# Where the row maximum of the attention scores is kept: an SBUF tile of its own, or a spare column of the scores' PSUM tile

## The chip, the cores and the metric

The kernel runs on 1 core of one Trainium2 chip. The metric is the device time of one execution in microseconds (us); several runs are taken and their median is compared. All times below come from those runs or from one profiled execution of the kernel.

## What is computed

Three layers follow each other over 4 batches of 576 tokens with 512 features. The first is attention with 8 heads of 64 features and a threshold: only scores within tau of the maximum of their row count.

```python
scores = scale * np.matmul(q, k.transpose(0, 1, 3, 2))
thresh = np.max(scores, axis=-1, keepdims=True) - tau
scores = np.where(scores >= thresh, scores, -1000000000.0)
attn = softmax(scores); x = np.matmul(attn, v)
```

Then each token goes through one of 8 experts (a gate picks one, or keeps the previous token's; two matrix products with a relu between, scaled by the expert's probability), and last through a normalised feed-forward layer with a residual. The change is in the attention alone.

## The kernel before, in words

Products are made on TensorE (PE) from float16 pairs (a high and a low part of each number). Attention goes pair of heads by pair of heads: 16 pairs (4 batches, 4 pairs each), nine *items* in each, 144 items in all. An item is 128 rows of queries against the 576 keys of their batch. Its scores are one PSUM tile `t` of the pool `ps_s`, 128 partitions by 2 by 512 float32 numbers. That is two banks, of which columns 0 to 287 are used in each. The pool has three such tiles.

The steps of an item, with their engine and the line of the code:

- `s_mm` (L342, L350, PE): the scores, four matmuls of 288 columns or twelve smaller ones.
- `mx` (L353 to L356, VectorE, DVE): the row maximum `m` of the 2 by 288 scores, by one reduction (L355).
- `bias` (L361, ScalarE, ACT): a copy of `m`, scaled, into column 0 of the small SBUF tile `bt`.
- `ex` (L367, ACT): the exponential `e` of the scores `t`, with `bt[:,0:1]` as bias.
- `thr` (L372, DVE): `bt[:,1:2] = m + ntau`, one number per partition; `ntau` is a constant in SBUF.
- `mask` (L382, for the odd item also L384, DVE): `em = (t >= threshold) * e`.
- `hilo` (L389 on ACT, L390 on GpSimd, POOL): `em` in two float16 parts `hl`.
- `tr` (L396): `hl` transposed by a DMA to `ht`, issued by SP; `pv` (L414 to L416, PE): times v; `norm` (L424, L428, L434, DVE): divided by the sum.

The order in which each engine gets its instructions is written out by hand in the loop that ends the kernel's attention part (L1038 to L1100). In step `it` of that loop `mx`, `bias` and `ex` belong to item `it`, then come `mask` of item `it - 1`, `thr` of item `it`, `hilo` of `it - 1` and `s_mm` of `it + 1`:

```python
if live: mx(*items[it])
...
    bias(*items[it])
...
    ex(*items[it])
if 0 < it <= NI:
    mask(*items[it - 1])
    if live: thr(*items[it])
```

So DVE's queue reads mx(it), mask(it-1), thr(it), other work, mx(it+1). ACT's reads bias(it), ex(it), hilo(it-1), other work, bias(it+1). Each engine takes its own queue strictly in order; between engines, semaphores hold an instruction until what it needs is there. The other work is dealt out by item number: scaling and splitting q, k and v of coming pairs (L295 to L329: ACT and POOL), narrowing of the feed-forward weights from 64-bit words (L154, L156, L158 on DVE, L169 and L176 on ACT, L170 on POOL), `norm`, the gate of a finished pair (L453 to L479) and, once a batch, the routing (L484 to L581, many small DVE operations). After the attention the experts and the feed-forward layer follow (L1103 to L1181), in which the change touches nothing.

Of the kernel before, what the change touches and what calls it, by code (L numbers as in the profile page):

```python
# [19 lines left out]
def kernel(  # L20
# [36 lines left out]
    x_d = dram.tile([NT, DM], F32, name="x_d")  # L57
    ys_d = dram.tile([NT, DM + 1], F32, name="ys_d")

# [1 line left out]
    ident = const.tile([128, 128], F32, name="ident")  # L61
    make_identity(nc, ident)
    ident16 = const.tile([128, 128], F16, name="ident16")
# [64 lines left out]
    nc.vector.tensor_tensor(out=taus, in0=t0, in1=ge, op=ALU.add)  # L128
    nc.vector.memset(c16, 16.0)

# [1 line left out]
    fw1 = fw_p.tile([128, 2, DM // 128, FF], F16, name="fw1")  # L132
    fw2 = fw_p.tile([128, 2, FF // 128, DM], F16, name="fw2")

# [4 lines left out]
    FA = 11  # L139

    def ffn_views(j):
        """1024 columns of float64 weights, as pairs of int32 words: source, place and scale."""
        if j < 8:
            c, o = j // 2, 1024 * (j % 2)
            src = w_ch1[128 * c:128 * c + 128, o:o + 1024].rearrange("p (a b) -> p a b", a=2)
            return src, fw1[:, :, c, o:o + 1024].rearrange("p t (a b) -> p t a b", a=2), g32[:, c:c + 1]
        j -= 8
        src = w_ch2[256 * j:256 * j + 256, :].rearrange("(c p) f -> p c f", p=128)
        return src, fw2[:, :, 2 * j:2 * j + 2, :], 64.0

    def narrow(t, r):
        """float64 words t to float32 r, in steps."""
        lo, hi = t[..., 0], t[..., 1]
        nc.vector.tensor_scalar(out=r, in0=hi, scalar1=3, scalar2=0x3FFFFFF8, op0=ALU.logical_shift_left, op1=ALU.bitwise_and)  # L154
        yield
        nc.vector.scalar_tensor_tensor(out=r, in0=hi, scalar=-(1 << 30), in1=r, op0=ALU.bitwise_and, op1=ALU.bitwise_or)  # L156
        yield
        nc.vector.scalar_tensor_tensor(out=r, in0=lo, scalar=29, in1=r, op0=ALU.logical_shift_right, op1=ALU.bitwise_or)  # L158
        yield

    def ffn_steps(j, a, cv_p):
        """the steps that load and split half of a part."""
        src, dst, scale = ffn_views(j)
        t = cv_p.tile([128, 512, 2], I32, name="stg")
        r = cv_p.tile([128, 512], I32, name="cv")
        rf = r.bitcast(F32)

        def low():
            nc.scalar.activation(out=dst[:, 0, a], in_=rf, func=AF.Copy)  # L169
            nc.gpsimd.tensor_tensor(out=dst[:, 1, a], in0=rf, in1=dst[:, 0, a], op=ALU.subtract)  # L170

        n = narrow(t, r)
        yield nc.sync.dma_start(out=t.rearrange("p b w -> p (b w)"), in_=src[:, a].bitcast(I32))
        for _ in range(3):
            yield next(n)
        yield nc.scalar.activation(out=rf, in_=rf, func=AF.Copy, scale=scale)  # L176
        yield low()

    def ffn_half(j, a):
        """the same for half of the columns; returns the step that follows the load."""  # L180
        src, dst, scale = ffn_views(j)
        t = P["sm2_p"].tile([128, 512, 2], I32, name="stg", tag="stg")
        nc.sync.dma_start(out=t.rearrange("p b w -> p (b w)"), in_=src[:, a].bitcast(I32))

        def run():
            r = P["n_p"].tile([128, 512], I32, name="xn", tag="xn")
            for _ in narrow(t, r):
                pass
            yield
            r = r.bitcast(F32)  # L190
            nc.scalar.activation(out=r, in_=r, func=AF.Copy, scale=scale)
            nc.scalar.activation(out=dst[:, 0, a], in_=r, func=AF.Copy)
            nc.gpsimd.tensor_tensor(out=dst[:, 1, a], in0=r, in1=dst[:, 0, a], op=ALU.subtract)

        return run()
# [1 line left out]
    P, wt = {}, {}  # L197

    def weights(u, n):
        """the tile of a unit's first (0) or second (1) weights."""  # L200
        if (u, n) not in wt:
            sh = [128, 2, DM // 128, F] if n == 0 else [128, 2, F // 128, DM]
            nm = f"w{n}{u % 2}"
            wt[u, n] = P["wb_p" if u % 2 else "wa_p"][n].tile(sh, F16, name=nm, tag=nm)
        return wt[u, n]

    def unit_part(u, j, p, ev):
        """loads the j-th eighth of a unit's weights; returns the step that splits it."""
        one = bass.ds(ev, 1) if not isinstance(ev, int) else slice(ev, ev + 1)
        t = p.tile([128, F], F32, name="stg", tag="stg")  # L210
        if j < 4:
            nc.sync.dma_start(out=t, in_=w1[one, 128 * j:128 * j + 128].rearrange("o p f -> p (o f)"))
            return lambda: split(weights(u, 0), t, j, 64.0)
        j -= 4
        t = t.rearrange("p (b f) -> p b f", f=DM)
        nc.sync.dma_start(out=t, in_=w2[one, 256 * j:256 * j + 256].rearrange("o (c p) f -> p (o c) f", p=128))
        return lambda: split(weights(u, 1), t, slice(2 * j, 2 * j + 2), 64.0)

    # ================= attention and routing =================
    R = dict(side="right")  # L220
    c_raw, c_tab, c_unit, c_tail, c_cv, c_pv, c_main = (ExitStack() for _ in range(7))
    tm = pool(c_tab, "tm", 1, **R)
# [19 lines left out]
    if True:  # L242
# [30 lines left out]
        pending, ops = {}, {}  # L273

        def load(b, nm, part):
            """one of four transfers of a batch's q, k or v."""
            src = {"q": q, "k": k, "v": v}[nm][b]
            o, m = (6, 1) if nm == "v" else (5, 0)
            t = raws[nm]
            if part < 2:  # L280
                n = NP // 2
                (nc.scalar if b else nc.sync).dma_start(
                    out=t[:, n * part:n * part + n].rearrange("p n (h r) d -> p (n h) (r d)", h=2)[:, :, 0:4 * D],
                    in_=src[2 * n * part:2 * n * part + 2 * n, 0:512].rearrange("h (p r) d -> p h (r d)", r=4))
            else:
                ab = part - 2
                (nc.scalar if b else nc.sync).dma_start(
                    out=t[64 * ab:64 * ab + 64, :, 4 + ab * m, :],
                    in_=src.rearrange("(n a) s d -> a s n d", a=2)[ab, 512:S])
# [61 lines left out]
            mst[s, ab] = t  # L351

        def mx(s, ab):  # L353
            m = sm_p.tile([128, 1], F32, name="m")
            nc.vector.tensor_reduce(out=m, in_=mst[s, ab][:, :, 0:288], op=ALU.max, axis=AX.XY)  # L355
            mst[s, ab] = (mst[s, ab], m)  # L356

        def bias(s, ab):
            t, m = mst[s, ab]
# [85 lines left out]
            nc.scalar.dma_start(out=x_d[b * S + 512:b * S + S, cols], in_=xc[0:64, 4, :])  # L445

        def bank(b):
            """a bank for small products; at the end, when there are more, one of those."""
            if b == B - 1 and "pa" in P:
                return P["pa"].tile([128, 4, 128], F32, name="a")  # L450
            return ps_t.tile([128, 4, 128], F32, name="t")

        def gate(p):  # L453
            """x of a head pair, transposed, for the logits."""
            b, hp = divmod(p, NP)
            xc = xcs[p]
            xt = xts[p % 2]
# [24 lines left out]
                yield from route(b)  # L482

        def route(b):  # L484
            """experts, their probabilities and places of a batch's tokens."""
            lg, e1 = lgs[b % 2], e1s[b % 2]
            T = lambda nm, sh, dt=F32: rt_p.tile(sh, dt, name=nm)
            V = nc.vector
# [92 lines left out]
                early_tables()  # L581

        def early_tables():
            """tables of the first tiles of two experts, without the last batch."""
            V = nc.vector
            V.tensor_scalar(out=etb, in0=acc[:, 0, 0:2], scalar1=OFF + NT / 2, scalar2=None, op0=ALU.add)
            V.tensor_scalar(out=etp, in0=acc[:, 1, 0:2], scalar1=2.0 ** -33, scalar2=None, op0=ALU.mult)
# [39 lines left out]
        for b in range(1, B):  # L627
            for o, a in zip(LO, (("q", 0), ("k", 0), ("v", 0), ("q", 2), ("q", 3), ("k", 2), ("k", 3), ("v", 2), ("v", 3), ("q", 1), ("k", 1), ("v", 1))):
                at(36 * (b - 1) + o, load, b, *a)
    # ================= tables of the units =================  # L630
    V = nc.vector

    def static_tables():
# [86 lines left out]
        V.tensor_scalar(out=P["tb"][:, 2 * E:NC], in0=A[:, 0:NDYN], scalar1=OFF + NT / 2, scalar2=None, op0=ALU.add)  # L720
        V.tensor_scalar(out=P["tp"][:, 2 * E:NC], in0=A[:, NDYN:2 * NDYN], scalar1=2.0 ** -33, scalar2=None, op0=ALU.mult)

    # ================= experts and feed-forward =================
    parts, wsel, us = {}, {}, {}

    PAIRS = {"a": (0, 1), "b": (2, 3)}

    def tiles(u):
        """table columns of a unit: two tiles of an expert's first rows, or one tile."""
        if u in PAIRS:  # L730
            return PAIRS[u]
        return (2 * u, 2 * u + 1) if u < E else (E + u,)
# [12 lines left out]
            us[u, "g"].append(xg)  # L745

    def fetch(u, j):
        """the j-th eighth of a unit's weights."""
        if u not in wsel:
            if u < E:  # L750
                wsel[u] = u
# [23 lines left out]
    late = []  # L775

    def drip(n=1):
        """splits the next parts of the weights, and loads ahead."""
        if late:
            next(late.pop(), None)  # L780
        for _ in range(n):
# [15 lines left out]
            more()  # L797

    def pace(u, share):
        """a share of the steps up to the end of a unit's part of the queue."""  # L800
        n = 0
        for k in pq:
            if k[0] != "f" and (k[0] - u) * 8 + k[1] > (7 if u < 6 else 11):
# [12 lines left out]
        us[u, "x"] = P["u_p"].tile([128, 2, 2, 4, 128], F16, name="xT")  # L816

    def t_unit(u):
        """x of a unit's tokens, transposed on the tensor engine."""
        new_x(u)  # L820
        x = us[u, "x"]
        for n, xg in enumerate(us.pop((u, "g"))):
# [4 lines left out]
            V.scalar_tensor_tensor(out=x[:, 1, n], in0=t, scalar=64.0, in1=x[:, 0, n], op0=ALU.mult, op1=ALU.subtract)  # L827

    def n_unit(u):
        """x of a unit's tokens in two float16 parts."""  # L830
        xs = us.pop((u, "g"))
        xn = P["n_p"].tile([128, 2, 2, DM], F16, name="n16")
        for n, xg in enumerate(xs):
# [2 lines left out]
        us[u, "n"] = xn  # L836

    def x_unit(u):
        """and transposed by the DMA engines."""
        new_x(u)  # L840
        x, xn = us[u, "x"], us.pop((u, "n"))
        if not single(u):
# [3 lines left out]
                nc.sync.dma_start_transpose(out=x[:, a, 0], in_=xn[:, a, 0])  # L846

    def s1_steps(u, k):
        """a part of the first product: as many columns as a bank holds."""
        x = us[u, "x"]  # L850
        two = u in PAIRS
        i, k = divmod(k, 2) if two else (0, k)
# [55 lines left out]
            pass  # L908

    def early_work():  # L910
        """the first tiles of two experts, in steps."""
        t_unit("a")
        yield
        for _ in range(4):
# [85 lines left out]
    NG = NT // 256  # L1000

    def halve(h):
        """half of the work of two sorted tiles."""
        g, b = divmod(h, 2)
        if b == 0:
            for fb in range(8):
# [204 lines left out]
```

## Time and profile before

| | us |
|---|---|
| median of 3 runs | 1118.63 |
| fastest and slowest run | 1113.96, 1120.94 |
| span of the profiled execution, first to last instruction | 1116.4 |
| attention: first and last row maximum start | 18.9, 421.5 |

For the profiled execution only its span is given, not a time of its own. The median of the runs is 2.2 us above the span; the span plus that is taken as the time of the profiled execution.

In the rows below, a group of instructions is one line: line of the code, engine, operation, names of what it writes and reads, shapes, count, busy time in us, mean duration of one in ns, and the idle time of the engine just before them with what ended it. Rows of the timeline begin with start and duration in us; an idle time before the instruction and what ended it stand in square brackets. A successor can start some hundredths before the predecessor's end, since engines overlap them.

### The profile page before, as it was taken

Reading aid. Unit: us, or ns where it says so; the run is one execution under the profiler, and the core shown is the slowest. Engines: PE = TensorE matmul, PEld = TensorE weight load, DVE = VectorE, ACT = ScalarE, POOL = GpSimd, SP = SyncE. Lnnn points to the kernel's source line nnn. Section 1 sums busy time; section 2 is a strip of 40 time slices with the busy share of each in tenths; the row PEclk is TensorE's granted clock in tenths of the full one; section 3 lists DMA queues with packets and bytes.
Section 4 is the critical chain, followed back from the end, with each engine's and each line's share of the span. In section 5 each row is a group of like instructions: output and inputs, shape, how many; then the busy total and the mean of one; then the engine's idle time right before and its main releaser. Section 6 shows DMA issues by size and latency. Waiting matters only on the chain. (4 is left out here: it accounts for less than half of the span.)

```text
span 1116.4 us, 20698 instructions
## 1 busy us (share of the span) xinstructions
PE 908.6 (81%) x8136; PEld 645.9 (58%) x8136; DVE 690.3 (62%) x1321; ACT 536.7 (48%) x930; POOL 382.7 (34%) x329
## 2 busy tenths in 40 slices
PE   1667575766577677878998879999989999999997
PEld 0446453645456566555666548667575675675673
DVE  4989789999998985876557665647230321321320
ACT  4868676877588764544557554435120111110110
POOL 3768675777577661132223221110100000000000
PEclk9767775887588877998999998999999999999999
DMA  7999999999999989648879887646111102101100
GB/s 201 203 217 226 213 220 211 202 233 222 197 192 209 189 174 266 228 121 268 291 231 307 251 233 234 177 134 195 64 43 43 29 29 57 29 29 58 29 11 19
DMA packets 314075, 181.02 MB, mean 162 GB/s; under 512 B 259179, under 2 KB 280683, under 8 KB 313969
## 3 DMA queue, kind: packets, MB, share of 16 engines
q1 hardware_dynamic: 283296, 150.08, 58.3%
q10 hardware_dynamic: 25712, 15.36, 5.4%
q0 software_dynamic: 4960, 14.17, 3.7%
q8 instruction: 65, 1.06, 0.4%
q14 instruction: 42, 0.34, 0.1%
HBM read 100.17 MB, written 15.22 MB: 103 GB/s over the span
## 5 line engine op out<-in xcount | busy, mean ns | idle before, releaser
L390 POOL TENSOR_TENSOR hl<-em,hl 128x576 f16<-128x576 f32 x144 | 193.5, 1346 | 114.6 <-ACT hl L389 103.9
L991 PE MATMUL y<-fw,hid 128*128 128x512 f16 x864 | 190.8, 383 | 3.5 <-ACTq L1163 3.5
L978 PE MATMUL a<-nT,fw 128*128 128x256 f16 x1728 | 190.1, 273 | 0.0
L978 PEld LDWEIGHTS <-fw 128*128 128x128 f16 x1728 | 169.1, 98 | 21.5
L869 PE MATMUL a<-xT,w 128*128 128x128 f16 (+1 forms) x1536 | 131.4, 250 | 34.9 <-DMA xT<-n 30.6
L137 DVE SCALAR_TENSOR_TENSOR w<-stg,w 128x1024 f16<-128x1024 f32 x112 | 136.3, 1238 | 32.8 <-ACT w L136 31.9
L414 PE MATMUL o<-vh,ht 128*128 128x65 f16 (+1 forms) x790 | 106.4, 218 | 57.3 <-DMA ht<-hl 32.6
L981 ACT ACTIVATE hid<-a 128x512 f16<-128x512 f32 x72 | 42.7, 593 | 219.2 <-PE a L978 219.2
L869 PEld LDWEIGHTS <-w 128*128 128x128 f16 x1536 | 118.5, 103 | 49.7 <-DMA xT<-n 34.0
L991 PEld LDWEIGHTS <-hid 128*128 128x128 f16 x864 | 85.3, 99 | 106.2 <-issue 7.5
L342 PE MATMUL s<-qkt 128*128 128x288 f16 x256 | 90.1, 362 | 57.1 <-DVE em L382 25.7
L414 PEld LDWEIGHTS <-ht 128*128 128x128 f16 (+1 forms) x800 | 89.8, 116 | 71.8 <-DMA ht<-hl 41.6
L382 DVE SCALAR_TENSOR_TENSOR em<-s,bt,e 128x576 f32<-128x576 f32 x144 | 115.6, 803 | 20.4 <-POOL hl L390 12.2
L996 POOL DMA_INDIRECT out_dram<-xf x18 | 18.9, 1049 | 317.1 <-DVE xf L995 317.1
L136 ACT ACTIVATE w<-stg 128x1024 f16<-128x1024 f32 x112 | 113.8, 1047 | 16.6 <-DMA stg<-in_moe_w_dram 12.6
L890 PE MATMUL y<-w,hid 128*128 128x512 f16 x528 | 118.8, 383 | 0.3 <-DVE w L137 0.3
L355 DVE TENSOR_REDUCE m<-s 128x1 f32<-128x576 f32 x144 | 107.3, 745 | 6.3 <-PE s L342 6.0
L982 DVE SCALAR_TENSOR_TENSOR hid<-a,hid 128x512 f16<-128x512 f32 x72 | 49.5, 688 | 99.3 <-ACT hid L981 97.8
L389 ACT ACTIVATE hl<-em 128x576 f16<-128x576 f32 x144 | 98.1, 681 | 23.3 <-DMA ht<-hl 16.4
L367 ACT ACTIVATE e<-s,bt 128x576 f32<-128x576 f32 x144 | 106.6, 740 | 4.7
L342 PEld LDWEIGHTS <-qkt 128*128 128x128 f16 x512 | 53.6, 121 | 94.6 <-DVE em L382 42.9
L995 DVE SCALAR_TENSOR_TENSOR xf<-y,xf 128x512 f32<-128x512 f32 x18 | 12.5, 692 | 153.1 <-PE y L991 153.1
(253 smaller groups left out, 1440.4 us busy)
## 6 DMA issues: line engine op xcount, KB each, us to landing
stg<-in_moe_w_dram SPq DMA_DIRECT2D x112, 512.0 KB
stg<-in_moe_w_ch_dram SPq DMA_DIRECT2D x32, 512.0 KB
xf<-ys_d SPq DMA_DIRECT2D x9, 513.0 KB
ku<-qkt SPq DMA_DIRECT2D x30, 144.0 KB
x_d<-xc ACTq DMA_DIRECT2D x16, 256.0 KB
rawq<-in_q_dram ACTq DMA_DIRECT2D x6, 512.0 KB
rawk<-in_k_dram ACTq DMA_DIRECT2D x6, 512.0 KB
vraw<-in_v_dram ACTq DMA_DIRECT2D x6, 512.0 KB
```

Source lines behind the costliest of these rows:

```text
L136: nc.scalar.activation(out=dst[:, 0, n], in_=t, func=AF.Copy, scale=scale)
L137: nc.vector.scalar_tensor_tensor(out=dst[:, 1, n], in0=t, scalar=scale, in1=dst[:, 0, n], op0=ALU.mult, op1=ALU.subtract)
L342: nc.tensor.matmul(t[:, c, 0:288], w, kk[:, 576 * ab + 288 * c:576 * ab + 288 * c + 288], start=(n == 0), stop=(n == 1))
L355: nc.vector.tensor_reduce(out=m, in_=mst[s, ab][:, :, 0:288], op=ALU.max, axis=AX.XY)
L367: nc.scalar.activation(out=e, in_=t[:, :, 0:288], func=AF.Exp, bias=bt[:, 0:1], scale=SC)
L382: nc.vector.scalar_tensor_tensor(out=o, in0=t[:, :, 0:288], scalar=th, in1=e, op0=ALU.is_ge, op1=ALU.mult)
L390: nc.gpsimd.tensor_tensor(out=hl[:, 1, c], in0=em[:, c], in1=hl[:, 0, c], op=ALU.subtract)
L414: mm(o[:, 0:65], ht[:, 0, j, sl], vh[:, jv, 0:65], start=(c == 0), stop=False)
L869: nc.tensor.matmul(ps[:, f, :], t1[:, a, c, fc], x[:, h, i:i + N // 128, c, :], start=(n == 0), stop=(n == 11))
L890: nc.tensor.matmul(ps, hid[:, x, f, 128 * i:128 * i + 128], t2[:, a, f, :], start=(n == 0), stop=(n == 23))
L978: nc.tensor.matmul(ps[:, f, :], fw1[:, a, c, fc], x[:, h, :, c, :], start=(n == 0), stop=(n == 11))
L991: nc.tensor.matmul(ps, hid[:, x, f, ts_], fw2[:, a, f, :], start=(n == 0), stop=(n == 47))
```

## The change

The maximum `m` is no longer a tile of the SBUF pool `sm_p`; it is the last column, 511, of the second bank of the item's own scores tile, which no matmul writes and no other step reads. The reduction writes there; `bias` (ACT) and `thr` (DVE) read it there. `sm_p` has one kind of tile less; nothing else is moved.

```diff
         def mx(s, ab):
-            m = sm_p.tile([128, 1], F32, name="m")
-            nc.vector.tensor_reduce(out=m, in_=mst[s, ab][:, :, 0:288], op=ALU.max, axis=AX.XY)
-            mst[s, ab] = (mst[s, ab], m)
+            t = mst[s, ab]
+            m = t[:, 1, 511:512]
+            nc.vector.tensor_reduce(out=m, in_=t[:, :, 0:288], op=ALU.max, axis=AX.XY)
+            mst[s, ab] = (t, m)
```

The rest of the diff takes out comments and docstrings.

## Rows read from the trace of the kernel before

**Rows 1.** The page of the profile: its first line
```profile
span 1116.4 us, 20698 instructions
```

**Rows 2.** Busy time by stretch, the attention: stretch, length, PE, PEld, DVE, ACT, POOL, clock, DMA share, GB/s
```profile
18.00:425.00 407.00, 269.49 (x3286) 209.49 (x3286) 370.98 (x774) 302.96 (x597) 279.05 (x214) 0.74 1.07 209
```

**Rows 3.** Groups of instructions of the whole span, by line
```profile
L355 DVE TENSOR_REDUCE m<-s 128x1 f32<-128x576 f32 x144 | 107.3, 745 | 6.3 <-PE s L342 6.0
L367 ACT ACTIVATE e<-s,bt 128x576 f32<-128x576 f32 x144 | 106.6, 740 | 4.7
...
L372 DVE TENSOR_TENSOR bt<-m,ntau 128x1 f32<-128x1 f32 x144 | 75.6, 525 | 0.0
...
L361 ACT ACTIVATE bt<-m 128x1 f32<-128x1 f32 x144 | 28.5, 198 | 63.1 <-DVE m L355 62.5
```

**Rows 4.** One line's instructions, L372: shortest, median, longest in ns, first and last start
```profile
L372 DVE TENSOR_TENSOR bt<-m,ntau x144: 138/476/1264, 19.7 to 422.9; 128x1 f32<-128x1 f32 x144
```

**Rows 5.** Timeline of DVE, ends of the nine items from 240.07, one whole
```profile
240.07 0.74 DVE L355 TENSOR_REDUCE m<-s 128x1 f32<-128x576 f32 x1
...
248.26 0.74 DVE L355 TENSOR_REDUCE m<-s 128x1 f32<-128x576 f32 x1
248.93 0.80 DVE L382 SCALAR_TENSOR_TENSOR em<-s,bt,e 128x576 f32<-128x576 f32 x1
249.66 1.15 DVE L372 TENSOR_TENSOR bt<-m,ntau 128x1 f32<-128x1 f32 x1
250.73 0.19 DVE L479 TENSOR_TENSOR lg<-t,lg 128x45 f32<-128x45 f32 x1
250.84 0.74 DVE L355 TENSOR_REDUCE m<-s 128x1 f32<-128x576 f32 x1
...
262.45 0.74 DVE L355 TENSOR_REDUCE m<-s 128x1 f32<-128x576 f32 x1
```

**Rows 6.** Timeline of POOL beside the whole item of rows 5
```profile
249.43 1.35 POOL L329 TENSOR_TENSOR vl<-vraw,vh 128x640 f16<-128x640 f32 x1
250.74 1.27 POOL L390 TENSOR_TENSOR hl<-em,hl 128x576 f16<-128x576 f32 x1
```

**Rows 7.** Timeline of ACT beside the whole item of rows 5
```profile
249.04 0.20 ACT L361 ACTIVATE bt<-m 128x1 f32<-128x1 f32 x1 [0.65 <-DVE m L355]
249.27 0.74 ACT L367 ACTIVATE e<-s,bt 128x576 f32<-128x576 f32 x1
249.91 0.67 ACT L389 ACTIVATE hl<-em 128x576 f16<-128x576 f32 x1
251.62 0.20 ACT L361 ACTIVATE bt<-m 128x1 f32<-128x1 f32 x1 [1.03 <-DVE m L355]
```

**Rows 8.** Single lines of DVE: shortest, median, longest in ns, first and last start
```profile
L434 DVE TENSOR_TENSOR xc<-o,rd x47: 273/410/425, 45.7 to 434.3; 128x256 f32<-128x256 f32 x32, 64x128 f32<-64x128 f32 x15
...
L479 DVE TENSOR_TENSOR lg<-t,lg x10: 192/193/195, 114.3 to 424.4; 128x45 f32<-128x45 f32 x10
...
L424 DVE TENSOR_SCALAR rd<-o x47: 138/145/163, 44.1 to 433.9; 128x4 f32<-128x4 f32 x32, 64x2 f32<-64x2 f32 x15
...
L158 DVE SCALAR_TENSOR_TENSOR cv<-stg,cv x22: 676/1386/1651, 32.1 to 310.7; 128x512 int32<-128x512 int32 x22
```

**Rows 9.** Two lines of ACT, from PSUM and from SBUF: ns, first and last start
```profile
L462 ACT ACTIVATE xt<-t x15: 576/585/597, 74.6 to 425.4; 128x512 f32<-128x512 f32 x15
...
L176 ACT ACTIVATE cv<-cv x6: 612/612/619, 245.5 to 314.4; 128x512 f32<-128x512 f32 x6
```

**Rows 10.** Who waited for whom, 60 to 420 us: us in total, times, longest
```profile
ACT bt L361 <- DVE m L355: 50.9, 56, 2.5
...
ACT hl L389 <- DMA ht<-hl: 16.4, 5, 6.4
...
ACT nat L301 <- DMA qkt<-nat: 8.3, 2, 4.5
```

## The prediction, made before the changed kernel was run

> **What bounds the kernel now.** I read the page first, then busy time by stretch, then the groups of instructions, then single lines and the timelines of DVE, ACT and POOL for one pair of heads, and last the waits. The span is 1116.4 us [rows 1], and the part that the change touches is the attention, 18 to 425 us. There DVE is busy 371.0 of 407 us (91%), ACT 303.0 (74%), POOL 279.1 (69%), PE 269.5; the DMA engines show a share of 1.07, so their queues are hardly ever empty [rows 2]. DVE sets the pace: in the nine items from 240.07 its rows follow each other without a gap (the whole item shown in [rows 5] is an example), while ACT stands idle before L361 until DVE's maximum is there, 50.9 us in 56 waits [rows 10]. The expert stage behind starts when the attention is done, so what the attention gains or loses moves the end one for one.
>
> Within DVE one row is odd. L372, an addition of one number per partition, takes 138 ns at best, 476 at the median and 1264 at worst [rows 4]; its 144 instructions add up to 75.6 us [rows 3]. In the item shown it starts at 249.66, takes 1.15 and ends at 250.81; POOL's operation beside it ends at 249.43 + 1.35 = 250.78 [rows 5, 6]. I laid all 144 against POOL's timeline: 87 last 0.2 us or more, and 83 of these end within 0.06 us of the end of a POOL operation. So an L372 that meets a running POOL operation waits for its end, inside its own duration. Both its inputs, m and ntau, lie in SBUF. L479 and L434 are additions and products of the same kind with one input in PSUM and one in SBUF: 192 to 195 ns, and 410 at the median with 425 at most [rows 8], never stretched, although the L479 shown starts at 250.73 just as POOL's next operation does [rows 5, 6].
>
> **The change part by part.**
>
> *The stretched additions go.* With m in PSUM L372 is like L479. 144 x 0.138 = 19.9 us stay of 75.6; -55.7 us on DVE's queue.
>
> *Their reading from PSUM.* L424 reads PSUM, 4 elements, in 145 ns at the median [rows 8] against 138: +7 ns, 144 times, +1 us. The bounds are -1 and, by its longest 163 ns, +3.6; I take +1, L424 being the nearest row. [...] The sum here goes by the row.
>
> *The reduction's output.* No DVE instruction of the trace writes PSUM. The nearest row is L355 itself, 745 ns into SBUF [rows 3]. By the difference that reading shows, the bound is some 25 ns either way (L424 shortest against longest), 144 x 0.025 = +-3.6 us. I take 0.
>
> *bias gets cheaper.* ACT's copy of 512 elements takes 585 ns from PSUM (L462) and 612 from SBUF (L176) [rows 9]: about -0.03 us per item. It lies between mx and ex, so today it is hidden behind DVE's mask; what it is worth depends on the next step.
>
> *A new meeting on one PSUM bank.* m now lies in the bank that ex is reading. ex(it) reads it on ACT while DVE comes to thr(it). In the item shown the maximum ends at 249.00, bias and ex fill ACT to 250.01, and thr starts at 249.66 [rows 5, 7]. Today, of all readers of s, the reduction ends before ex starts and mask starts after ex has ended. I take it that the program keeps these two apart as well, with thr held until ex has ended, in the order of the code. Behind a held thr on DVE stand all the other work and the next maximum, and for that wait bias, ex and all of ACT. [...]
>
> What the hold costs, from the nine items 240.07 to 262.45 [rows 5]. Today they take 22.38 us; L372's stretch is 3.4 us of that. With the hold the loop from one end of ex to the next has two branches, and the longer counts. DVE's: 0.05 for the semaphore, 0.07 to the successor of thr, D us of other DVE work, 0.74 for the maximum, 0.04 to bias: 0.90 + D. ACT's: hilo and other work H, less 0.10, by which a successor starts before ex's end [rows 7]. Then bias and ex, 0.97 today, 0.94 with the cheaper bias. From the two timelines D is 0, 1.66, 0.54, 0.12, 1.23, 0, 0.35, 0.34, 0.61 (the fourth is the item shown, with L479 alone) and H is 1.74, 1.67, 1.20, 0.57, 1.66, 1.72, 1.06, 0.57, 1.31 (the fourth is L389 alone). The longer branches are 1.64, 2.56, 1.44, 1.02, 2.13, 1.62, 1.25, 1.24, 1.51, together 14.41; with 9 x 0.94 it makes 22.87, against 22.38. So the hold takes back the 3.4 us and 0.5 more. For 16 pairs of heads: +8 us, with the -55.7 already in it, as is the cheaper bias.
>
> *What else moves.* L158, two SBUF inputs, is stretched as well: 1386 ns at the median against 676, some 9.7 us over 22 of them. With the hold it comes right after ex's end, when POOL's L390 hasn't begun; but the other POOL operations can still meet it: between 0 and -9.7, I take half, -5. When ACT waits for a DMA (16.4 us in 5 waits for ht, 8.3 in 2 for qkt [rows 10]), DVE today runs on through one mask and one maximum, 0.72 + 0.67 = 1.4 us. A held thr stops it before that. At most 7 x 1.4 = +10, and below nothing if the DMAs, with more time per item, are late less often. I take +3.
>
> Sum: +8 + 1 - 5 + 3 = +7 us on the span of 1116.4, 1123.4. With the 2.2 us by which the median of the runs stands above the span: about 1125. It is also what a large gain and a large cost leave over, so the sign is not sure.
>
> **The rivals.**
>
> *No hold: faster.* If thr isn't kept behind ex, the nine items cost DVE 9 x 1.46 (0.67 + 0.72 + 0.07) + 4.85 (the sum of D) + 0.6 of norm = 18.6, and ACT 9 x 0.84 + 11.5 (the sum of H) = 19.1, against 22.38. That is 3.3 a pair, 52 us over 16. But the DMA share is over 1 [rows 2] and DMA waits are there already; two thirds, -35, seem to be the most likely: 1084. For it: the code orders thr by nothing but m. Against it: two engines reading one bank at once is nowhere in the trace.
>
> *The hold costs more: slower.* Summed over the 144 items, ex ends 104.5 us after the start of thr (137 times later than it). If all of that fell on the end, 104.5 - 55.7 = +49, 1168. DVE's own slack and the ACT branch hide a part. With half of it, +25: 1143. It decides once the step from one maximum to the next, 2.80 us now ((421.5 - 18.9) / 143), is above 2.88. For it: ACT's lateness would reach DVE at once, where a mask and a maximum cover it now. Against it: the nine items worked above.
>
> *The port is still taken: slower.* If L372 is stretched with one input in SBUF too, the hold comes on top: +50, 1168. L479 and L434 speak against it.
>
> **How the numbers follow.** Forecast (held, nearly balanced) 0.55, its own range 1112 to 1136; no hold 0.17; the hold costs more 0.23; port still taken 0.05. About 1% is what a measurement of this kernel can tell from no change: 1107.4 to 1129.8. Faster takes the 0.17 and 0.02 of the forecast's lower edge, 0.19. Within 1% lies 0.42 of the forecast. Slower has the remaining 0.11 of the forecast, 0.23 and 0.05, 0.39. The range reaches down towards the first rival without its full gain and up past the second: 1094 to 1148.
>
> **What would show it.** Right: L372 close to 140 to 145 ns at every percentile and no stretch; in the waits, DVE's L372 waiting for ACT's ex (L367) in most of the 144 items, some 60 us in all; DVE's busy time in the attention down by about 55 us with the end of the attention hardly moved; L361 near 170 ns instead of 198 [rows 3]. Wrong: no wait of L372 on L367 and an attention that ends 30 us earlier (first rival), or an attention that ends over 20 us later with ACT idle before L361 as now (second), or L372 still up to 1.2 us (third). If the reduction is longer than 745 ns by more than 25, the term that I set to 0 was wrong.

## The result, and the profile after

The changed kernel takes 1131.51 us at the median of 4 runs (1127.50 to 1134.13), the kernel before 1118.78 (1113.96 to 1120.94). The ratio is 1.012, with a 95% interval from 1.0088 to 1.0152: slower by 13 us. Its profiled execution spans 1130.7 us, 14.3 more than that of [rows 1]. All of it lies in the attention. The last row maximum starts at 436.4 us instead of 421.5, the first at 19.3 instead of 18.9, so the attention is 14.5 us longer and the rest unchanged. From here on lines behind L355 count one more than before: L372 has become L373, L361 L362, L367 L368.

The groups of instructions of the changed kernel that answer to [rows 3], in the same columns:

```profile
L362 ACT ACTIVATE bt<-s 128x1 f32<-128x1 f32 x144 | 24.0, 167 | 83.0 <-DVE s L356 79.9 <-DVE rd L425 2.6
L373 DVE TENSOR_TENSOR bt<-s,ntau 128x1 f32<-128x1 f32 x144 | 22.6, 157 | 58.7 <-ACT e L368 57.0 <-issue 0.3
```

L373 has gone from 75.6 us busy to 22.6. In exchange it has an idle time in front of it, which it did not have at all: 57.0 us, ended by ACT's ex. The single line, which answers to [rows 4] (columns: shortest, median, longest in ns, first and last start; below it what its engine waited for, us in total and times):

```profile
L373 DVE TENSOR_TENSOR bt<-s,ntau x144: 140/158/160, 21.1 to 438.1; 128x1 f32<-128x1 f32 x144
...
  ACT e L368: 57.0, 109
```

None of these 144 additions is stretched any more, and 109 of them wait for ex. Busy time by stretch, the changed kernel's row for the stretch of [rows 2]:

```profile
18.00:425.00 407.00, 265.44 (x3120) 205.32 (x3119) 328.03 (x743) 291.80 (x576) 267.06 (x205) 0.70 1.03 200
```

In this stretch DVE is busy 43 us less and stands still that much more; a part of that is work which now falls behind 425 us. Over the whole execution DVE's busy time fell by 31 us (690.3 to 659.5), though L373 alone gave up 53: other instructions of DVE took longer. TensorE's granted clock, a mean over parts at 1.00 and parts at 0.50 (in the changed kernel 1.00 from 39 to 45 us, 0.50 from 46 to 76), was 0.70 in the stretch against 0.74, and PE got fewer matmuls done (3120 against 3286).

Who waited for whom between 60 and 420 us, the rows that answer to [rows 10]:

```profile
ACT bt L362 <- DVE s L356: 64.7, 63, 3.2
DVE bt L373 <- ACT e L368: 46.9, 90, 2.8
```

DVE now waits for ACT, and ACT waits for DVE more than before (64.7 us against 50.9): the two take turns. ACT's waits for the DMAs became shorter in this execution: at most 3.1 us instead of 6.4 for ht, 2.2 in all instead of 8.3 for qkt.

Where the 14.5 us lie is seen from the starts of the row maxima, pair of heads by pair (nine items each; differences after less before, us): pairs 6, 10 and 14, under which a batch's routing runs on DVE, are longer by 4.3, 4.5 and 3.2, together 12.0. Pairs 2, 4 and 5, in which DMAs were late, are shorter by 1.1, 2.9 and 3.0. The other ten add up to +9.3. The routing pairs repeat: 4.3, 4.5 and 3.3 in the trace of `mix_in`, an experiment below. The others change with the execution: pairs 2, 4 and 5 are 7.4 us shorter there as well, though they keep m in SBUF as before.

### The profile page after: what moved, and what is told of

Its sections match the earlier page's. It is cut to its first block, busy times and chain, and to the rows that moved or that the text cites. A ratio compares the mean times of both kernels' runs of the same rounds, so it can differ in the third digit from the quotient of the medians.

```text
span 1130.7 us, 20451 instructions
## 1 busy us (share of the span) xinstructions
PE 915.5 (81%) x8136; PEld 650.8 (58%) x8136; DVE 659.5 (58%) x1321; ACT 536.3 (47%) x930; POOL 381.8 (34%) x329
## 3 DMA queue, kind: packets, MB, share of 16 engines
q8 instruction: 65, 1.06, 0.4%
## 5 line engine op out<-in xcount | busy, mean ns | idle before, releaser
L391 POOL TENSOR_TENSOR hl<-em,hl 128x576 f16<-128x576 f32 x144 | 191.1, 1329 | 137.2 <-ACT hl L390 122.6
L415 PE MATMUL o<-vh,ht 128*128 128x65 f16 (+1 forms) x790 | 111.1, 222 | 58.4 <-DVE xc L435 28.4
L342 PE MATMUL s<-qkt 128*128 128x288 f16 x256 | 93.0, 372 | 58.2 <-DVE em L383 31.1
L415 PEld LDWEIGHTS <-ht 128*128 128x128 f16 (+1 forms) x800 | 93.0, 119 | 73.4 <-issue 38.4
L997 POOL DMA_INDIRECT out_dram<-xf x18 | 18.9, 1052 | 317.0 <-DVE xf L996 317.0
L356 DVE TENSOR_REDUCE s<-s 128x1 f32<-128x576 f32 x144 | 108.9, 756 | 5.4 <-PE s L342 5.4
L416 PE MATMUL o<-vl,ht 128*128 128x64 f16 (+1 forms) x790 | 111.0, 220 | 0.0
L417 PE MATMUL o<-vh,ht 128*128 128x65 f16 (+1 forms) x790 | 110.9, 221 | 0.0
L368 ACT ACTIVATE e<-s,bt 128x576 f32<-128x576 f32 x144 | 106.6, 741 | 4.7
```

The lines of the kernel that those rows point to most:

```text
L342: nc.tensor.matmul(t[:, c, 0:288], w, kk[:, 576 * ab + 288 * c:576 * ab + 288 * c + 288], start=(n == 0), stop=(n == 1))
L391: nc.gpsimd.tensor_tensor(out=hl[:, 1, c], in0=em[:, c], in1=hl[:, 0, c], op=ALU.subtract)
L415: mm(o[:, 0:65], ht[:, 0, j, sl], vh[:, jv, 0:65], start=(c == 0), stop=False)
L416: mm(o[:, 0:64], ht[:, 0, j, sl], vl[:, jv, :], start=False, stop=False)
L417: mm(o[:, 0:65], ht[:, 1, j, sl], vh[:, jv, 0:65], start=False, stop=(c == 4))
```

## The experiments

Two properties were to be taken apart: whether the small addition is stretched by POOL (called *the port*: taken or free), and whether thr waits for ex (*the hold*). The kernel before has the first alone, the changed kernel the second alone. Ratios, with their 95% intervals, are to the kernel before in the same batch of runs (its medians were 1118.83, 1117.16 and 1118.31 us), and they are not exactly the quotients of the medians shown.

**Without the hold.** Three ways. `ps_late` and `ps_early` keep m in PSUM and move thr alone:

```diff
 # ps_late
             if live: mx(*items[it])
+            if 0 < it <= NI: thr(*items[it - 1])
...
-                if it == 0: thr(*items[it])
-                if live: thr(*items[it])
 # ps_early
-            if live: mx(*items[it])
+            if live:
+                mx(*items[it])
+                thr(*items[it])
...
-                if it == 0: thr(*items[it])
-                if live: thr(*items[it])
```

In `ps_early` the tile `bt` is then made in thr and handed on to bias, since thr comes first.

> The changed kernel with one thing moved: thr of an item is issued one step later on DVE, right behind the next item's maximum and ahead of its own mask. Theory (the hold behind ex costs what the freed port gains): by then ex has nearly always ended, so L373 waits for ex under 10 us in all instead of 57, and its instructions stay near 140 to 160 ns; 1080 to 1105 us, faster than both kernels. Rival (the hold is not what costs; the slower maximum and addition in PSUM do, and DVE does not set the pace): 1125 to 1135, as the changed kernel.

Measured: 1117.0 us, ratio 0.9992 (0.9964 to 1.0020), between the two ranges.

> The changed kernel with thr issued right behind the item's own maximum, ahead of bias and ex. Theory (hold): DVE no longer waits for ex; instead bias waits for thr, some 0.15 to 0.25 us per item on the way from the maximum to ex, partly where ACT is late anyway; 1090 to 1120 us, faster than the changed kernel. Rival (hold is not what costs): 1125 to 1135.

Measured: 1112.32 us, ratio 0.9978 (0.9940 to 1.0016). The third leaves m in SBUF and takes the second tensor away:

```diff
 # sb_scalar, on the kernel before
-            nc.vector.tensor_tensor(out=bt[:, 1:2], in0=m, in1=ntau, op=ALU.add)
+            nc.vector.tensor_scalar(out=bt[:, 1:2], in0=m, scalar1=ntau, scalar2=None, op0=ALU.add)
```

> The kernel before with m in SBUF, where thr adds ntau as a number per partition (tensor_scalar) instead of as a second tensor; no meeting with ex on a bank, so no hold. Theory: if that takes the stretch away (L372 under 0.2 us nearly always), it is the port's relief alone: 1075 to 1100 us. If the number per partition still goes through what POOL holds, the median of L372 stays near 476 ns and the time at 1115 to 1123. Rival (DVE does not set the pace): stretch gone and still 1113 to 1123.

Measured: 1115.11 us, ratio 0.9958 (0.9928 to 0.9988). Its line of the addition, and that of `ps_late` (columns as above):

```profile
L372 DVE TENSOR_SCALAR bt<-m,ntau x144: 192/204/213, 19.8 to 418.6; 128x1 f32<-128x1 f32 x144
```
```profile
L373 DVE TENSOR_TENSOR bt<-s,ntau x144: 136/150/160, 20.8 to 418.9; 128x1 f32<-128x1 f32 x144
...
  ACT e L368: 27.6, 19
```

So the stretch of this addition is gone in both, in `sb_scalar` with both operands in SBUF, one of them given as a number per partition. The hold is not quite gone in `ps_late`: 19 items still wait, 27.6 us in all where under 10 were expected. All three are 14 us or more faster than the changed kernel: without most of the hold, or without any, its loss is gone. `ps_late` and `sb_scalar` do not reach the 1075 to 1105 us that were expected (`ps_early` lies in its range): the freed port is worth 1 to 5 us. For `sb_scalar` the rival came true, the stretch gone and still 1113 to 1123. DVE is not all that sets the pace.

**The hold alone.** One element of e is named as an operand that does not enter the result:

```diff
 # sb_hold, on the kernel before
-            nc.vector.tensor_tensor(out=bt[:, 1:2], in0=m, in1=ntau, op=ALU.add)
+            nc.vector.scalar_tensor_tensor(out=bt[:, 1:2], in0=m, scalar=e[:, 1, 287:288], in1=ntau, op0=ALU.bypass, op1=ALU.add)
```

> The kernel before with m in SBUF and two tensor inputs, where thr also names one element of e as a number per partition that does not enter the result, so that it has to wait for ex: the hold alone. Theory: L372 waits for ex some 50 to 60 us in all as in the changed kernel, and its instructions are stretched as before or somewhat less (20 to 55 us in all); 1140 to 1185 us. Rival (hold is not what costs): 1115 to 1125.

Measured: 1146.31 us, ratio 1.0254 (1.0204 to 1.0305), 28 us slower. Its line:

```profile
L372 DVE SCALAR_TENSOR_TENSOR bt<-m,e,ntau x144: 200/220/3284, 21.1 to 453.8; 128x1 f32<-128x1 f32 x144
...
  ACT e L367: 47.6, 108
```

The wait (47.6 us, 108 times) is nearly that of the changed kernel. The median of 220 against a shortest of 200 shows that, held, the addition seldom meets a POOL operation (35 of the 144 still do and are stretched). This operation is 60 ns dearer than the one of before, 9 us over 144, which is part of the 28. So the hold costs some 20 to 28 us with the port shared and about 18 with it free (1.012 against 0.9958 of 1118.8). The changed kernel pays the hold and gets back a part through the freed port.

**Why the freed port pays so little.** One part of the answer is DVE itself. The busy times of the engines over the whole execution, from the pages of the kernel before and of `sb_scalar`:

```profile
PE 908.6 (81%) x8136; PEld 645.9 (58%) x8136; DVE 690.3 (62%) x1321; ACT 536.7 (48%) x930; POOL 382.7 (34%) x329
```
```profile
PE 904.2 (81%) x8136; PEld 642.3 (58%) x8136; DVE 669.7 (60%) x1321; ACT 535.2 (48%) x930; POOL 385.3 (35%) x329
```

DVE's busy time falls by only 21 us (24 in `ps_late`, 20 in `ps_early`), though the addition itself takes 46 to 54 us less. The narrowing of the weights (L154, L156, L158, 48.7 us before) takes 63 to 65 us in these three kernels: it meets POOL's operations in the addition's place (of these 66 instructions 12 were stretched before; in the trace of `light_scalar`, below, it is 39, and all 39 start beside a running POOL operation).

The other part is the DMAs. Between 60 and 420 us PE waits for the transposed attention weights in the kernel before and in `sb_scalar`

```profile
PE o L414 <- DMA ht<-hl: 30.4, 13, 6.6
```
```profile
PE o L414 <- DMA ht<-hl: 46.7, 23, 4.3
```

So the transposes were halved, in three kernels alike (here in the changed one), which leaves the low parts of the attention weights out of the result:

```diff
 # light_after; the same two lines in light_before and light_scalar
-            nc.sync.dma_start_transpose(out=t.rearrange("p a b c -> p (a b) c"), in_=hl.rearrange("p a b -> p (a b)"))
+            nc.sync.dma_start_transpose(out=t[:, 0], in_=hl[:, 0])
...
-                    mm(o[:, 0:65], ht[:, 1, j, sl], vh[:, jv, 0:65], start=False, stop=(c == 4))
+                    mm(o[:, 0:65], ht[:, 0, j, sl], vh[:, jv, 0:65], start=False, stop=(c == 4))
```

> The kernel before, where the DMA transposes only the high part of em (half of the bytes of L396); pv takes the high part again in place of the low one, so the low parts of the attention weights are left out. Theory (with the port free, the next limit is the DMA transposes): here DVE with its stretched additions is the limit, so a small gain, 1095 to 1115 us; waits for ht nearly gone. Rival (the limit behind DVE is not the DMA): 1112 to 1120.

> The kernel with m in SBUF and thr as tensor_scalar, with the same half of the transposes and the same low parts left out. Theory (DMA is what kept the freed port from paying): now it pays, 25 to 45 us below light_before, 1055 to 1085 us. Rival (another limit): within 8 us of light_before.

> The changed kernel, with the same half of the transposes and the same low parts left out. Theory (hold and freed port nearly cancel where no DMA is late, and the routing adds some 12 us): within -5 to +20 us of light_before, and 25 to 60 us above light_scalar. Rival (another limit than DMA): as far above light_scalar as the changed kernel stands above its sibling now, 10 to 20 us.

Measured: light_before 1092.37 us (0.9767, 0.9692 to 0.9843), light_scalar 1073.67 (0.9608, 0.9539 to 0.9678), light_after 1109.54 (0.9935, 0.9904 to 0.9966). In all three PE's waits for ht are nearly gone: 1.2 us at most where 30.4 and 46.7 stood. Busy time by stretch of the first two, in this order (columns as in [rows 2]):

```profile
18.00:425.00 407.00, 275.72 (x3492) 217.38 (x3492) 385.43 (x803) 314.95 (x613) 278.89 (x215) 0.79 0.80 172
```
```profile
18.00:425.00 407.00, 283.44 (x3660) 221.72 (x3660) 378.22 (x851) 321.29 (x625) 287.32 (x219) 0.82 0.83 183
```

With the DMA share at 0.75 (light_after) to 0.83 instead of 1.03 to 1.07, the freed port alone brings 19 us (1092.4 to 1073.7) where it had brought 4 to 5, and the hold with the freed port costs 36 (1109.5 to 1073.7) where it had cost about 18. DVE's busy time falls by 26 us here (692.2 to 665.9), little more than the 21 without the halving, so it is the transposes that had kept most of DVE's gain from the time. The expected 25 to 45 was a little high, the direction is clear: in the kernel as it is, the transposes cap what DVE can gain, and hide a part of what it loses. The halving alone brings the kernel before 25 us, more than the small gain expected of light_before (1095 to 1115): the DMAs limited it too. light_after lies where it was expected.

**Where the hold hurts.** Two kernels keep m in PSUM for some pairs of heads only:

```diff
 # mix_in; mix_out has "not in"
-            m = t[:, 1, 511:512]
+            m = t[:, 1, 511:512] if s // 5 in (6, 10, 14) else sm_p.tile([128, 1], F32, name="m")
```

> m in PSUM only in the three pairs of heads (6, 10, 14) under which the routing of a batch runs on DVE; in the other thirteen m stays in SBUF as before. Theory (the loss sits in the routing stretches, where DVE alone is the path, L372 was not stretched and the hold comes on top): nearly the whole loss, 8 to 14 us above the kernel before, 1127 to 1133. Rival (the loss is spread evenly over the 16 pairs): 3/16 of 12.7 us, 1120 to 1123.

Measured: 1132.67 us, ratio 1.0145 (1.0071 to 1.0220), from four runs between 1122.74 and 1135.56; its trace is of the shortest.

> The reverse of mix_in: m in PSUM in the thirteen pairs without routing, in SBUF in pairs 6, 10 and 14. Theory (the loss sits in the routing stretches; elsewhere hold, freed port and shorter DMA waits cancel): within 5 us of the kernel before. Rival (the loss is spread over the pairs): 13/16 of 12.7 us, 8 to 12 us slower than before.

Measured: 1116.41 us, ratio 0.9984 (0.9958 to 1.0010). With 27 items in PSUM the whole loss is there, with the other 117 none. The traces agree: pairs 6, 10 and 14 are together 12.2 us longer than before in `mix_in`, as in the changed kernel, and 0.9 in `mix_out`. TensorE's clock does not explain it: over 18 to 425 us it was 0.74 in `mix_in`, as in the kernel before, and 0.882 and 0.883 over the whole execution. The waits say the reverse. The group of the PSUM items' addition in `mix_out` is

```profile
L373 DVE TENSOR_TENSOR bt<-s,ntau 128x1 f32<-128x1 f32 x117 | 18.4, 157 | 56.6 <-ACT e L368 55.7
```

55.7 us of waiting that cost nothing, while the same group of `mix_in` shows

```profile
L373 DVE TENSOR_TENSOR bt<-s,ntau 128x1 f32<-128x1 f32 x27 | 4.2, 157 | 5.4 <-ACT e L368 4.9
```

4.9 us and the whole loss. What happens in a routing pair is seen in the timeline of DVE. One item of the kernel before, pair 6:

```profile
186.19 0.81 DVE L382 SCALAR_TENSOR_TENSOR em<-s,bt,e 128x576 f32<-128x576 f32 x1
186.92 0.15 DVE L372 TENSOR_TENSOR bt<-m,ntau 128x1 f32<-128x1 f32 x1
...
187.81 0.20 DVE L544 TENSOR_TENSOR rk<-rk,oh 128x40 f32<-128x40 f32 x1
...
188.16 1.11 DVE L548 TENSOR_TENSOR val<-pe,val 128x5 f16<-128x5 f32 x1
```

and the same item of the changed kernel, with POOL's operation beside it in the second fence:

```profile
187.70 0.81 DVE L383 SCALAR_TENSOR_TENSOR em<-s,bt,e 128x576 f32<-128x576 f32 x1
188.80 0.16 DVE L373 TENSOR_TENSOR bt<-s,ntau 128x1 f32<-128x1 f32 x1 [0.29 <-ACT e L368]
...
189.70 1.06 DVE L545 TENSOR_TENSOR rk<-rk,oh 128x40 f32<-128x40 f32 x1
...
190.90 0.16 DVE L549 TENSOR_TENSOR val<-pe,val 128x5 f16<-128x5 f32 x1
```
```profile
189.42 1.28 POOL L391 TENSOR_TENSOR hl<-em,hl 128x576 f16<-128x576 f32 x1 [2.60 <-ACT hl L390]
```

thr starts 1.10 us after the start of the mask instead of 0.73: 0.37 us in this item for a wait of 0.29. It was not stretched before either, so there is nothing to gain. And stretches move among the routing's operations: its own product of two SBUF tensors (rk) takes 1.06 us instead of 0.20, ending (190.76) just behind POOL's operation (190.70), while the subtraction L548, stretched to 1.11 us before, takes 0.16. In this item the two cancel; in the whole pair they do not. Over the nine items of pair 6 four routing operations (the scan of loc, oh, rk and oc) take 4.1 us more, three others (val, ov and ex) 1.4 less and L373 0.9 less. DVE runs the same 72 instructions in the same order in both kernels, so the 4.3 us of this pair can be split: 2.2 lie between mask and thr, the hold, and 2.1 are stretches that other operations took on, net of those that went. In pair 10 it is 2.2 and 2.3, in pair 14, where L372 had been stretched in three items, 2.7 and 0.5.

**Order alone, and the best version.** `ps_early` was run again with more rounds, beside `sb_early`, which makes the same move of thr with m in SBUF.

> ps_early once more, with more rounds: m in PSUM and thr right behind the maximum. It was 0.9978 of the kernel before with an interval that holds 1. Theory (port free, no hold, limited by the DMA transposes): 2 to 8 us faster than before. Rival (the wait of bias for thr eats the gain): no difference.

Measured: 1113.32 us, ratio 0.9934 (0.9903 to 0.9966).

> The kernel before with m in SBUF, where only thr is moved, right behind the item's maximum: the order of ps_early without the freed port. Theory: L372 is stretched as before (median some 0.3 to 0.6 us) and stands ahead of the mask; 0 to 10 us slower than ps_early, 1114 to 1125. Rival (the order alone makes ps_early what it is): as fast as ps_early.

Measured: 1120.41 us, ratio 1.0019 (0.9992 to 1.0045). Its addition is stretched nearly as before, 459 ns at the mean and 66.1 us in all (525 and 75.6 before).

So neither the place in PSUM (as the change has it) nor the order alone helps; both together bring 7 us by the second ratio (5 between the medians), where the first (0.9978, an interval that holds 1) could not tell it from nothing. `ps_early` and `sb_scalar` are the two versions that beat both kernels, the kernel before by under 1%.

## Why the prediction was right or wrong

*The stretched additions: right for the line, not for DVE.* 53.0 us were taken off L372 (75.6 to 22.6); the forecast had 55.7 less 1. (Of the 87 long ones the prediction counted 83 that end within 0.06 us of the end of a POOL operation; in the trace it is all 87.) But DVE's busy time fell by 31 us over the execution, not by the 55 named among the signs: that a stretch taken off one instruction comes back in others was not in the sum.

*The PSUM operands: small, as by the rows.* The addition's median is 158 ns, 20 over the old shortest, where L424 had suggested 7: 3 us in all instead of 1, within the bounds. The reduction into PSUM takes 756 ns instead of 745, 1.6 us in all, set to 0 with a bound of 3.6. bias fell from 198 to 167 ns, as forecast.

*The hold: there, and its waiting right.* Some 60 us of L373 waiting for ex were forecast, 57.0 came, in 109 items, and no run without the hold shows the loss. (In the trace of the changed kernel all 144 additions start 0.03 us or more after the end of their ex; what unordered access would do was not tried.)

*The step that failed: "For 16 pairs of heads: +8 us".* Nine items without late DMAs and without routing were multiplied by 16. Two things were wrong in it. First, these nine items themselves took longer than 22.87 us: 24.39 us, 2.0 more than before where 0.5 was forecast (24.40 in light_after; 23.63 in `mix_out`, which has the same code there; 22.38 again in `mix_in`, which has that of before). The two branches held well: of the nine steps from one end of ex to the next, six came within 0.11 us of the forecast. The other three are

| forecast, us | measured | why |
|---|---|---|
| 3.50 | 2.78 | L158 no longer stretched: 0.68 instead of 1.39 |
| 2.38 | 3.43 | DVE's norm waits 0.7 for PE's product with v, and behind it ACT's hilo 0.8 for the mask |
| 3.07 | 4.13 | L158 stretched instead: 1.65 instead of 0.69 |

So PE and stretches that move were left out. Why PE was late there stays open: `mix_out` has no such wait at the same granted clock, 0.72, and light_after has it at a DMA share of 0.69, so neither the clock nor late DMAs account for it.

Second, the routing pairs, 12.0 of 14.5 us, are not like these nine items: DVE alone is the path there, L372 had hardly been stretched, so the hold had little to be set against, and the stretch went over to the routing's operations. `mix_in` and `mix_out` show that the loss sits there. For the other thirteen pairs the balance of hold and freed port was right within what the runs can tell: no loss in `mix_out`, and between the traces of light_before and light_after, where late DMAs do not blur it, 3.4 us in thirteen pairs, beside 13.0 in the three with routing.

*The DMA waits: not settled.* +3 us were forecast for what DVE can no longer do while ACT waits for a DMA. Pairs 2, 4 and 5 became 7 us shorter instead, but that cannot be put down to the change: with m in SBUF, as before, they are shorter too (7.4 us in `mix_in`, 9.0 in `sb_early`). The traced execution of the kernel before had its DMAs late there. *L158: nothing came.* -5 us were forecast; its 22 instructions take 1167 ns each at the mean instead of 1128, for it still meets POOL's other operations, and with L154 and L156 the narrowing takes 4.4 us more than before.

In sum +7 was forecast and +14.3 came on the span. The sign and the mechanism held; that the sum came so near is in part luck. Nine items at +2.0, multiplied by 16, would have given +32; the routing, 12 us, was in no term; and the other pairs lost next to nothing.

*The second rival: half of it came.* By the prediction's own threshold it decides once the step from one maximum to the next is above 2.88 us. The step was 2.82 before (stated as 2.80) and became 2.92. Its other sign, an attention that ends over 20 us later, did not come: 15 us. The time lies 6.5 us above the forecast and 11.5 below this rival's 1143.

*The first rival's price: wrong.* -35 us for a freed port without a hold; measured -1 to -7. Two things were too high in it. The 52 us were to come off DVE, but its busy time fell by only 20 to 24 us without the hold, since the weights' narrowing was stretched in the addition's place. And two thirds had been let through against a DMA share over 1; 1 to 7 of these 20 to 24 came through, and the halved transposes, where 19 of 26 did, show what held the rest back.

## What to carry to other kernels

The scalar that was moved into a spare column of the scores' PSUM tile also moved into that tile's order of access: 109 of its 144 additions waited for ex, 57.0 us in all, and none before. So look who else reads the tile at that moment, and move its reader to a place in the queue where the others are done. Here that gave back the loss and little more. The sum of a wait in the profile is not its price: 55.7 us cost nothing in thirteen pairs of heads, where DVE, ACT and the DMAs shared the pace, and 4.9 us beside three routing stretches went with a loss of 16. A stretch taken off one instruction can come back in the next one that meets the same engine (here 46 to 54 us came off the addition and 20 to 24 off DVE), so read the engine's whole busy time and not the line's alone. When large terms cancel, work out each kind of stretch by itself before multiplying one of them.

## What the runs showed of the hardware that was not expected

A DVE addition of one element per partition, with all operands in SBUF, was not stretched by POOL when one operand was given as a number per partition: 192 to 213 ns in 144 instructions, 91 of which start beside a running POOL operation, against 138 to 1264 with two tensors. The operand costs some 55 to 60 ns (at the shortest 192 here and 200 in `sb_hold`, against 138). This is not so for every operation with such an operand. In the same trace of `sb_scalar` this one, of two elements per partition, ends 0.03 us behind POOL's:

```profile
393.42 1.10 DVE L591 TENSOR_SCALAR ebad<-er,pidx 128x2 f32<-128x2 f32 x1
```
```profile
393.22 1.27 POOL L390 TENSOR_TENSOR hl<-em,hl 128x576 f16<-128x576 f32 x1 [2.81 <-ACT hl L389]
```

Whether the number of elements makes the difference was not tried. And freeing one instruction from POOL does not remove the conflict: other DVE operations on SBUF tensors then met POOL's and were stretched in its place: in the trace of `light_scalar` L156 took up to 1.72 us, beside a POOL operation, where it had taken 0.68 in the kernel before.
